# A gated mix of a spectral filter and a state-space scan: a new written order for all five engines

## The chip, the cores and the metric

The kernel runs on one core of one Trainium2 chip. The core has five engines with a queue each: TensorE (PE in the profile, its weight loads PEld), VectorE (DVE), ScalarE (ACT), GpSimd (POOL) and SyncE (SP, which here issues only transfers). The metric is the device time of one execution in microseconds, as the median of three runs. Lower is better. Inputs and outputs are bf16 in HBM.

## The reference

The input x has 2048 tokens of 1024 features. Two branches are computed and mixed by a gate that has one value for each token:

```
g = sigmoid((x * gate_w).sum(-1))
a = irfft2(rfft2(x) * (w_r + 1j*w_i))          # over tokens and features
Bu = x @ B_bar.T ; h[t] = Lam_bar * h[t-1] + Bu[t]   # 1024 complex states, 2048 steps
b = 2 * real(h @ C.T) + x * Dskip
out = g * a + (1 - g) * b
```

Lam_bar and B_bar come from Lambda, log_dt and B. Branch a is the spectral one, branch b the state-space one.

## The kernel before

**Branch b.** Tokens are worked on in 8 chunks of 256. For each chunk four unit steps (unit_mm, L398) multiply the chunk of x with B, 32 matmuls of 128x256 each, into a PSUM tile psu; unit_out (L408) casts it on ACT into the state buffer h. The recurrence on DVE (recur, L347 to L378: rotate, scan, carry, rotate back) is cut into 126 pieces. Then each tile of 128 tokens is multiplied with C: a half-tile step (c_half, L713) is 16 matmuls of 128x512 and fills 512 of the 1024 columns of the PSUM tile ps_y. ACT scales each half by 1 − g into a buffer ye (scale_y, L744; two buffers). For tokens tiles 0 to 9 ("early") SP stores ye to a scratch in HBM (L754), and the skip term x·Dskip is added to it there: DVE multiplies (L769), ACT scales into the buffers su (L779, one pair for all tiles), and POOL issues an accumulating transfer (add_skip, L785). For tiles 10 to 12 ("own") the skip term comes in through four short diagonal matmuls (L719), and POOL adds ye onto branch a with an accumulating transfer (own_add, L884). Tiles 13 to 15 are done last in pieces (c_part, L727) and finished on DVE (L899) and stored (L905).

**Branch a.** The two-dimensional transform goes in steps: transposes of x on PE (L917) and folds on DVE (L943 to L954), a transform over features (fd, L430 to L443, evicted at L449), a first step over tokens (s1, L462, evicted at L474, the last four of 16 into A_last), and a store to a first scratch (L480). From there come 8 tiles Bb in two halves each (load_mid, L508); s2 (L594) transforms them, ACT evicts to X (L603, with one column fixed at L604 by a result of the small chain "middle", L525 to L582), DVE multiplies with W (times_w, L617; W arrives by load_W, L515, four transfers each for w_r and w_i), is1 (L629) transforms back, ACT evicts to C (L637), SP stores to a second scratch (L643). Then come load_last (L651), is2 (L661) with its eviction (L671), and for each token tile the last step (spectral_mm, L806 and L810, into ps_id), scaled by g on ACT (L817), joined on DVE (L825 to L846). POOL adds the scratch of branch b onto it with another accumulating transfer (add_late, L851), and SP stores the result (close, L859).

**Loads.** B is read with transposing transfers (L259), C with 16 of them (load_C, L702), half of these into a region that B or A used before. Db (L758) is Dskip spread over all partitions, xs (L763) a tile of x, K (L497), KRS (L1029) and MT (L499) are constants.

**What sets the order.** No scheduler decides anything: under the manual schedule each engine runs its instructions in the order in which the Python steps emit them. Each step is a generator, each has one letter, and the string ORDER says which generator advances next. The letter v takes the recurrence piece whose number comes next in PIECES. PSUM has four slots, each of the size of a tile of 128x1024 in f32, and SLOTS says which slot the next tile takes; a tile waits until the slot's tile before it has been read for the last time. A transfer of SP is given one of eight counters in turn, and waits until the transfer that had the counter before has landed; POOL's transfers have eight counters of their own.

```
for act in "".join(ORDER):
    if act == "v":
        piece(next(pieces))
    else:
        next(acts[act], None)
```

Letters used below: c load_C, Y load_skip, W load_W, L load_small (K, MT), M load_mid, 3 s2, 4 its eviction to X, n and o the early and own half-tile steps of C, N and O their ye, J the store of ye, h and H the unit step and its eviction, 6 and 7 is1 and its eviction to C, m the su, + the L785, B the L884, Q the L851, l and z spectral_mm and its eviction for tiles 0 to 9, D the store of a finished tile, e the gate's output with the sigmoid (L1014), t the tables with the sines (L1111).

Of the kernel before, what the change touches and what calls it, by code (L numbers as in the profile page):

```python
# [41 lines left out]
S1_DVE = (1, 4, 5)  # L42
CLOSES = (0, 1, 2, 3, 10, 4, 5, 11, 12, 6, 7, 8, 9)
PIECES = (
# [6 lines left out]
)  # L51
SLOTS = (
    "0123012310231023102310230123012031201312031203101230132031231031201312303312013213021021013010320130",
    "1220123203201320130130120321023120320321021023120312301230231201302303120",
)
MIRROR = (6, 7, 8, 9)
ORDER = (
    "xxxTVUVVVaTfVVrrUGTGG|Tfaaa|UafFffftafftUftxFEfTETUFffU22xSEkSTSTArxAfffUAUFTTEUfffUFbxwxbxbbTUEFbfE",
    "1bT~SSUfuFSFAUUUU2bbtbfAF1AtbbtrFttrbEffE11EbEh11SStbttfttttAg1~HtfufhA~tetFSSFrKHrtu1EAvfAEhtttvttt",
    "SSFtbbvvvAtEttH1Avthtftv1cttwv1tcthccctttvtcch~HFtvftHvvhuHtvfStEettStAHhtAeKrvFctcvvFhEEHKtvwtcSvtS",  # L60
    "hvvKc1vcc1vAAKKvv1c1v1hcvswcsLMvvveHHekMYsssnNHvvhHnsvvvJWWMvs3vsvNvvsssssnvssnvvs4NMvv4Njvhv553vhvv",
    "YvyJJL46H4vv5WWvhh5vvvMM78Jj7HHmn3nHvv8M44m6MnN77WW5jv+Yy5vvv3M845+mNY8nMJJMyvvv+467hvHMh5vN7N34vHmh",
    "4J8m+6n3h8v77HmH+55v4n64JMvNnMYy5vW83n+v7N474vJ568vYmmNJ7dh7NWj+v58v5vyvvd88MhvHHm8+MJm6h+n378vv7Hh8",
    "J+d4Y4YX5vv5NnJH6XXv7ny7mNNm8+hn8hvqivvvvvJvqyHihYivvyiqhivqqiYvNImvni+qJJmHIIiini+HinvdIIH+vvIIIqIN",
    "IiiiNmI+vvIInvvImvyJqii%NJINIJYJYmhvvv+vvvlylzvhHmplpzZZH+mZZZhlZvhPPRR++zyRRRlQDQHzRZZmRHZ+ZRZvoOZD",
    "QvlpDzzPovOvQBvZZlpPYvZZvBZDZRDRRRvzQDoloOBzoQOopZOoPOBlzlZRoDDZZvBZZRpQvzCvYZZvZZBZZPRDoQoo9RQQ9yRR",
    "0RRyCooD099C9Y990DD0D0Y00",
)

EVEN = ((0, 0), (2, 1), (2, 0), (0, 1))  # L70
# [1145 lines left out]
```

## Time and profile before

| | |
|---|---|
| median of 3 runs | 305.4 us (304.77, 305.4, 305.66) |
| span of the profiled execution | 303.6 us (the page gives no other time for it) |
| PE busy | 296.4 us (98%) |
| DVE busy | 289.3 us (95%) |
| ACT busy | 188.5 us (62%) |
| POOL busy | 73.3 us (24%) |
| granted TensorE clock | 0.999 |

The span is what lies between the first and the last instruction. A row of a group names the line, the engine, the operation, what is written and read, the count, and then the busy time, the mean duration of one in ns, and the idle time of the engine ahead of these instructions with what ended most of it. In a list by time, a row has start and duration, and a square bracket with the idle time before it. "DMA to landing" is the time from the start of an issue until the last packet has arrived. A wait by engine gives the total, the number of times and the longest.

### The profile page before, as it was taken

The page shows a single profiled execution, that of the slowest core. Times are in us where ns is not written, and L with a number is a line of the kernel's source. Part 1 is how long each engine was busy: PE and PEld are TensorE (multiplying, and loading weights), DVE is VectorE, ACT ScalarE, POOL GpSimd, SP SyncE. Part 2 cuts the span into 40 slices and gives each one's busy share as a digit, 9 for nine tenths or more (in the row PEclk, how much of TensorE's full clock was granted, in tenths as well). Part 3 has the DMA queues.
Part 4 walks back from the last instruction along what each step waited for, and adds up shares of the span by engine and source line. Part 5 has one row for each costly group of instructions (what it writes and reads, how often), then busy time and mean ns, then how long its engine had stood idle before and what let it go on. Part 6 is the DMA issues. An engine that isn't in the chain of part 4 may idle for free. (4 is left out here: it accounts for less than half of the span.)

```text
span 303.6 us, 6402 instructions
## 1 busy us (share of the span) xinstructions
PE 296.4 (98%) x2568; PEld 197.4 (65%) x2592; DVE 289.3 (95%) x340; ACT 188.5 (62%) x255; POOL 73.3 (24%) x99
## 2 busy tenths in 40 slices
PE   8999999999999999999999999999999999999995
PEld 5664677878864685458553866669657986645543
DVE  2999999999999999999999999999899999999995
ACT  4999999896532383667665865529668774343400
POOL 2100420745893001110210220202011253252330
PEclk9999999999999999999999999999999999999999
DMA  6999999989999599895948798687758876978976
GB/s 208 341 201 194 253 193 310 162 142 154 268 214 241 160 259 219 181 250 189 212 96 258 163 223 225 139 294 147 242 174 185 165 88 135 160 132 143 165 153 181
DMA packets 74157, 59.35 MB, mean 196 GB/s; under 512 B 44904, under 2 KB 61680, under 8 KB 74128
## 3 DMA queue, kind: packets, MB, share of 16 engines
q1 hardware_dynamic: 66560, 49.82, 65.8%
q0 software_dynamic: 6912, 8.69, 23.0%
q10 hardware_dynamic: 656, 0.44, 0.5%
q8 instruction: 20, 0.33, 0.4%
q14 instruction: 9, 0.07, 0.1%
HBM read 27.46 MB, written 23.08 MB: 166 GB/s over the span
## 5 line engine op out<-in xcount | busy, mean ns | idle before, releaser
L398 PE MATMUL psu<-xQ,BT 128*128 128x256 bf16 x1024 | 116.5, 273 | 0.2 <-DVE X L449 0.2
L398 PEld LDWEIGHTS <-BT 128*128 128x128 bf16 x1024 | 99.0, 98 | 17.3 <-issue 4.6
L713 PE MATMUL ps_y<-CT,h 128*128 128x512 bf16 x397 | 92.5, 379 | 0.9
L363 DVE TENSOR_TENSOR_SCAN h<-rz,h 128x2048 bf16<-128x2048 f32 (+1 forms) x20 | 70.8, 3561 | 0.0
L713 PEld LDWEIGHTS <-h 128*128 128x128 bf16 x416 | 39.6, 98 | 46.3 <-issue 2.9
L785 POOL DMA_DIRECT2D y_scratch<-su x20 | 17.3, 902 | 135.7 <-ACT su L779 105.4
L408 ACT CAST h<-psu 128x1024 bf16<-128x1024 f32 x32 | 32.3, 1011 | 18.7 <-PE psu L398 13.1
L350 DVE TENSOR_TENSOR h<-h,tab 128x4096 bf16<-128x4096 bf16 (+1 forms) x20 | 37.1, 1859 | 0.1
L744 ACT ACTIVATE ye<-ps_y,omg 128x512 f32<-128x512 f32 x26 | 17.9, 689 | 26.3 <-PE ps_y L713 11.8
L347 DVE TENSOR_TENSOR xQ<-h,tab 128x4096 bf16<-128x4096 bf16 x12 | 27.4, 2284 | 1.0 <-ACT h L408 1.0
L603 ACT CAST X<-ps_s 128x1024 bf16<-128x1024 f32 x16 | 16.2, 1010 | 14.6 <-PE ps_s L594 11.2
L727 PE MATMUL ps_q<-CT,h 128*128 128x512 bf16 (+2 forms) x110 | 21.3, 348 | 0.2
L817 ACT ACTIVATE BT<-ps_id,gB 128x1024 bf16<-128x1024 f32 x14 | 15.3, 1114 | 9.9 <-PE ps_id L810 5.7
L671 ACT CAST ZT<-ps_is 128x1024 bf16<-128x1024 f32 x16 | 15.8, 1017 | 6.2 <-PE ps_is L661 6.2
L637 ACT CAST C<-ps_is 128x1024 bf16<-128x1024 f32 x16 | 15.7, 1011 | 5.1 <-DMA xQ<-in_A_x_dram 3.4
L851 POOL DMA_DIRECT2D BT<-y_scratch x10 | 13.1, 1452 | 19.7 <-DVE BT L846 13.3
L727 PEld LDWEIGHTS <-h 128*128 128x128 bf16 x112 | 10.3, 98 | 10.4 <-DVE h L378 0.5
L779 ACT ACTIVATE su<-xs,omg 128x512 f32<-128x512 bf16 x20 | 14.2, 723 | 4.1 <-DMA y_scratch<-su 2.2
L929 ACT COPY xQ<-pt 128x1024 bf16<-128x1024 bf16 x12 | 12.2, 1082 | 1.3 <-PE pt L919 1.3
L449 ACT CAST X<-ps_fd 128x1024 bf16<-128x1024 f32 x12 | 12.3, 1062 | 1.0 <-PE ps_fd L439 0.9
L617 DVE TENSOR_TENSOR UV<-X,Wb 128x2048 bf16<-128x2048 bf16 x8 | 9.6, 1220 | 0.6 <-ACT ye L744 0.6
L617 DVE TENSOR_TENSOR UV<-X,raw 128x2048 bf16<-128x2048 bf16 x8 | 9.8, 1223 | 0.2 <-ACT X L604 0.2
(200 smaller groups left out, 397.3 us busy)
## 6 DMA issues: line engine op xcount, KB each, us to landing
y_scratch<-ye SPq DMA_DIRECT2D x20, 256.0 KB, 4.6
y_scratch<-su POOLq DMA_DIRECT2D x20, 256.0 KB, 4.7
Bb<-turn_scratch SPq DMA_DIRECT2D x16, 256.0 KB, 5.2
turn_scratch<-C SPq DMA_DIRECT2D x16, 256.0 KB, 4.1
raw<-turn_scratch SPq DMA_DIRECT2D x8, 512.0 KB, 4.3
xs<-in_A_x_dram SPq DMA_DIRECT2D x13, 256.0 KB, 3.9
out_dram<-BT SPq DMA_DIRECT2D x11, 256.0 KB, 4.3
CT<-in_A_x_dram SPq DMA_DIRECT2D x5, 512.0 KB, 6.1
```

The lines of the kernel that those rows point to most:

```text
L347: nc.vector.tensor_mul(out=tmps["s"], in0=u[:, ::-1], in1=bc(i))
L350: nc.vector.tensor_mul(out=u, in0=u, in1=bc(i))
L363: nc.vector.tensor_tensor_scan(out=seg, data0=rz[:, js.start + j:js.start + j + m].rearrange("p j t -> p (j t)"), data1=seg, initial=0.0, ...
L398: nc.tensor.matmul(psu[:, j, :], lhsT=BT[4 * q + j][:, ri, d8, :], rhs=xQ[:, c, d8, :], start=(d8 == 0), stop=(d8 == 7))
L408: nc.scalar.copy(out=hs[c][:, ri, 4 * q:4 * q + 4].rearrange("p b (q j) -> p b q j", j=32), in_=psus.pop((c, q, ri)).rearrange("p b (j q) ...
L603: nc.scalar.copy(out=X2, in_=ps2s[g][b])
L617: nc.vector.tensor_mul(out=UV, in0=X2s.pop((g, b)).unsqueeze(1).to_broadcast([P, 2, 2, K]), in1=fft["Wb"][g // 2 % 2][:, :, at:at + 1, :]. ...
L671: nc.scalar.copy(out=ZT[:, 4 * kp:4 * kp + 4, :, 4 * G:4 * G + 4].rearrange("p (c r) n g -> p c r n g", c=2), in_=pszs.pop((G, kp)).rearra ...
L713: nc.tensor.matmul(psy, lhsT=hs[c][:, ri, jb, P * tq:P * (tq + 1)], rhs=CT[ri][:, jb, 512 * dh:512 * (dh + 1)], start=(i == 0), stop=(i == ...
L727: nc.tensor.matmul(psq, lhsT=hs[c][:, ri, jb, P * tq:P * (tq + 1)], rhs=CT[ri][:, jb, at:at + n], start=(i == 0), stop=(i == 15))
L744: nc.scalar.activation(out=ye, in_=psys[tb][:, K * hf:K * (hf + 1)], func=ACT.Copy, scale=omg[:, tb:tb + 1])
L785: nc.gpsimd.dma_start(out=y_dram[tb, hf], in_=xgs[tb, hf], accum_op=ALU.add)
```

## The change

The three tables PIECES, SLOTS and ORDER get new contents, and nothing else is touched. The letters of ORDER are the same in number, so the same operations are issued, on the same engines, with the same operands, but in another sequence, and PSUM tiles take other slots. The number of activation-table loads on ACT follows from the order: in the old order the last sine comes ahead of the sigmoid, in the new one the sigmoid comes first, and there are four table loads in place of three.

Four stretches of the queues, as they are issued before and after. SP, from the last load of C on:

```
before: C load, K, Bb half 1, KRS, Bb half 2, Db, ye store, W w_r x4, W w_i x4, Bb x2, xs, ...
after:  C load, Db, W w_r x4, xs, K, Bb half 1, W w_i x4, raw w_r x4, Bb half 2, ye store, Bb, ye store, Bb, MT, ...
```

ACT, around the first s2 evictions (h is a unit eviction):

```
before: ... h, h, ye(tile 0), h, h, ye(tile 0), Zr, X, X column, ye(tile 1), X, X column, ye(tile 1), X ...
after:  ... h, h, h, h, ye(tile 0), ye(tile 0), Zr, ye(tile 1), X, X column, ye(tile 1), X, X column, X ...
```

POOL, from its accumulating transfers of branch b on:

```
before: L785 x19, L851 x2, L785, L851 x2, L884 x2 (tile 10), L851, L884 (11), L851, L884 (11), L884 (12), L851, L884 (12), L851 x3
after:  L785 x16, L851 x2, L884 (10), L785, L851 x2, L785, L884 (10), L785 x2, L884 (11), L851 x2, L884 (11), L884 (12), L851, L884 (12), L851 x3
```

PE and ACT at the own tiles. Before, the first ye of tile 10 stands between its two half-tile steps (with two ps_id steps of PE there as well), and tiles 11 and 12 have both half-tile steps ahead of their first ye. After, tile 10 has both half-tile steps first, and the first ye of tiles 11 and 12 stands between the two, with no other step of PE there (in the string: "oOBo" and "oQzQBDDDzRZOZRo"). ACT there, after:

```
after:  ... su(8) x2, ye(10), L817 x2, ye(10), L817 x4, su(9) x2, ye(11), ye(11), L817 x2, ye(12), ye(12), L817 x2
```

The diff:

```diff
@@ -42,29 +42,29 @@
 S1_DVE = (1, 4, 5)
 CLOSES = (0, 1, 2, 3, 10, 4, 5, 11, 12, 6, 7, 8, 9)
 PIECES = (
-    0, 1, 2, 3, 4, 5, 6, 8, 7, 9, 11, 10, 24, 25, 27, 26, 12, 13, 15, 14, 17, 16, 28, 18,
-    20, 21, 19, 23, 22, 30, 37, 38, 29, 40, 39, 50, 41, 31, 33, 34, 43, 35, 36, 42, 51, 44, 46, 45,
-    52, 32, 53, 47, 54, 48, 49, 56, 55, 63, 64, 66, 57, 59, 58, 60, 65, 61, 67, 62, 69, 68, 76, 77,
-    72, 70, 73, 79, 71, 78, 80, 75, 74, 82, 81, 83, 85, 89, 90, 86, 84, 91, 92, 87, 93, 94, 95, 98,
-    96, 88, 99, 102, 100, 103, 97, 104, 105, 106, 107, 108, 101, 111, 109, 112, 114, 113, 115, 116, 110, 118, 117, 119,
-    121, 120, 122, 123, 124, 125,
+    0, 1, 2, 3, 5, 4, 6, 8, 9, 7, 11, 10, 24, 25, 27, 26, 12, 13, 28, 30, 15, 14, 17, 16,
+    29, 20, 18, 21, 23, 22, 37, 38, 19, 39, 31, 50, 40, 33, 34, 41, 35, 42, 43, 36, 46, 44, 47, 51,
+    53, 49, 48, 45, 52, 32, 54, 55, 56, 63, 64, 66, 59, 57, 60, 62, 65, 58, 61, 67, 69, 68, 72, 76,
+    77, 79, 70, 73, 71, 78, 74, 80, 75, 82, 81, 83, 89, 90, 85, 86, 91, 84, 92, 87, 93, 95, 94, 96,
+    88, 98, 99, 102, 100, 103, 97, 101, 104, 105, 106, 108, 107, 111, 109, 112, 113, 114, 110, 115, 116, 118, 117, 119,
+    120, 121, 122, 123, 125, 124,
 )
 SLOTS = (
-    "0123012310231023102310230123012031201312031203101230132031231031201312303312013213021021013010320130",
-    "1220123203201320130130120321023120320321021023120312301230231201302303120",
+    "0123012302130123012301230123012031231023103120310231203201320323103210230201301230123023102302130230",
+    "1230232301302130213021310132013201320321032032102310231023102310321302130",
 )
 MIRROR = (6, 7, 8, 9)
 ORDER = (
-    "xxxTVUVVVaTfVVrrUGTGG|Tfaaa|UafFffftafftUftxFEfTETUFffU22xSEkSTSTArxAfffUAUFTTEUfffUFbxwxbxbbTUEFbfE",
-    "1bT~SSUfuFSFAUUUU2bbtbfAF1AtbbtrFttrbEffE11EbEh11SStbttfttttAg1~HtfufhA~tetFSSFrKHrtu1EAvfAEhtttvttt",
-    "SSFtbbvvvAtEttH1Avthtftv1cttwv1tcthccctttvtcch~HFtvftHvvhuHtvfStEettStAHhtAeKrvFctcvvFhEEHKtvwtcSvtS",
-    "hvvKc1vcc1vAAKKvv1c1v1hcvswcsLMvvveHHekMYsssnNHvvhHnsvvvJWWMvs3vsvNvvsssssnvssnvvs4NMvv4Njvhv553vhvv",
-    "YvyJJL46H4vv5WWvhh5vvvMM78Jj7HHmn3nHvv8M44m6MnN77WW5jv+Yy5vvv3M845+mNY8nMJJMyvvv+467hvHMh5vN7N34vHmh",
-    "4J8m+6n3h8v77HmH+55v4n64JMvNnMYy5vW83n+v7N474vJ568vYmmNJ7dh7NWj+v58v5vyvvd88MhvHHm8+MJm6h+n378vv7Hh8",
-    "J+d4Y4YX5vv5NnJH6XXv7ny7mNNm8+hn8hvqivvvvvJvqyHihYivvyiqhivqqiYvNImvni+qJJmHIIiini+HinvdIIH+vvIIIqIN",
-    "IiiiNmI+vvIInvvImvyJqii%NJINIJYJYmhvvv+vvvlylzvhHmplpzZZH+mZZZhlZvhPPRR++zyRRRlQDQHzRZZmRHZ+ZRZvoOZD",
-    "QvlpDzzPovOvQBvZZlpPYvZZvBZDZRDRRRvzQDoloOBzoQOopZOoPOBlzlZRoDDZZvBZZRpQvzCvYZZvZZBZZPRDoQoo9RQQ9yRR",
-    "0RRyCooD099C9Y990DD0D0Y00",
+    "GVVVVxxxaVaTUTTUUffffftGTG||UffftxVrFFfrakarrtTfffaaE2SxbFEEAUTSArUffTUTUFExxTUTTfUUFFx2SbfffEExASSf",
+    "~fAT1SAkuFfEFUUUUFUAFrEEtgetbbbbbbt11f~ttbffbbueetttEbhHSA2hbttttttt111frrH~tSffuvttvFEFEbbtthAvbvtt",
+    "tf1tttHSASAhfttK11ctttwvvfewttttvttttSAccchhccHe~HHvFESAvttthtFucccFwEvvvvEtHthHSASAvvvvh1Fc1111wScc",
+    "hvtvtEttvccSvAvh1A1cKKcssYvvvvvvsvHHvvKKvHWvKhYssnHvvvNsnNvvvvLsMnssWWMvjsJM3vJnMssLsNyssvs4vvhN5434",
+    "J5vv4MMHvhH677WjhY3Hv54vvvm88n+564vvv7nMyMMM3vJmN7MNh+J5454vHvvn68855WW7nN78vvmJNvvvvv+hHvj6787Yhm34",
+    "4y5vh5HHm+mMvMM3484YynJN867+5W7WM+hXM5344dJmnJ88+HNJnNJ677vjnNY3vvvvh5v45m+4vHv6587588h7yvh86vHhH787",
+    "Hvvmmvnvvddvv8vXqYhnyNiJJvnnIvNNYvJJiIvNhhvHHHqiviqqqyIiIIh+mvi+HvvIiiII+qvvvnivvqJmNviIImnN+viIiinI",
+    "mYiIIqiinIIdv%vvvy++m+m+JvNJllvvvvNhzhHzvYyHpPvYpPZZllZZRhZZRyzzRRZHhHXllRRZoompmJRRJvQQOZZvvDzDzpZZ",
+    "vBOvZZ+QQ+PYppPPyBlvPZZRRvZmZvRvvm++YoOBollODDoQzQBDDDzRZOZRoOBlZZvRzZZvQzZZCYZZRRZZBQQQo9oRR9RRYYDD",
+    "yy00CCDDo9oDD9o900oo90900",
 )
 
 EVEN = ((0, 0), (2, 1), (2, 0), (0, 1))
```

## The prediction

> **What bounds the kernel now.** I read the page's busy times first, then the stretches, the waits of TensorE, and the costliest groups.
>
> ```profile
> PE 296.4 (98%) x2568; PEld 197.4 (65%) x2592; DVE 289.3 (95%) x340; ACT 188.5 (62%) x255; POOL 73.3 (24%) x99
> ...
> PE   8999999999999999999999999999999999999995
> ...
> ACT  4999999896532383667665865529668774343400
> ```
> ```profile
> 0.00:50.00 50.00, 47.20 (x424) 31.93 (x428) 42.48 (x95) 44.22 (x60) 9.01 (x32) 1.00 1.05 241
> 50.00:100.00 50.00, 49.84 (x409) 36.47 (x411) 49.13 (x70) 30.48 (x46) 29.42 (x31) 1.00 1.12 199
> 100.00:200.00 100.00, 99.53 (x967) 62.38 (x975) 99.20 (x78) 61.58 (x89) 10.39 (x12) 1.00 0.82 203
> ```
> ```profile
> PE psw L987 <- DVE A L982: 1.2, 1, 1.2
> ...
> PE psu L398 <- DVE X L449: 0.2, 1, 0.2
> ```
> The second figure of a stretch is the busy time of PE. Of the first 50 us PE idles 2.80, of the next 150 only 0.63. Its waits are six rows of 2.7 us in all, the largest 1.2, the last 0.2. So the kernel is a row of matmuls without gaps. DVE (95%) is nearly as full. No operation is changed, so PE's own work stays, and two things alone can move the time: an order can win back at most the idle of the first 50 us, and every place where the new order lets PE wait adds its wait in full, since nothing later has slack to return it. (303.6 − 296.4 = 7.2 us of idle in all; about 3.2 of it is the tail after the last matmul, by the rows below.)
>
> ```profile
> 292.44 7.99 PE ps_q L727 x52
> ```
>
> Work beside PE, by group:
>
> ```profile
> L398 PE MATMUL psu<-xQ,BT 128*128 128x256 bf16 x1024 | 116.5, 273 | 0.2 <-DVE X L449 0.2
> ...
> L744 ACT ACTIVATE ye<-ps_y,omg 128x512 f32<-128x512 f32 x26 | 17.9, 689 | 26.3 <-PE ps_y L713 11.8
> ...
> L603 ACT CAST X<-ps_s 128x1024 bf16<-128x1024 f32 x16 | 16.2, 1010 | 14.6 <-PE ps_s L594 11.2
> ...
> L817 ACT ACTIVATE BT<-ps_id,gB 128x1024 bf16<-128x1024 f32 x14 | 15.3, 1114 | 9.9 <-PE ps_id L810 5.7
> ...
> L637 ACT CAST C<-ps_is 128x1024 bf16<-128x1024 f32 x16 | 15.7, 1011 | 5.1 <-DMA xQ<-in_A_x_dram 3.4
> ...
> L851 POOL DMA_DIRECT2D BT<-y_scratch x10 | 13.1, 1452 | 19.7 <-DVE BT L846 13.3
> ...
> L779 ACT ACTIVATE su<-xs,omg 128x512 f32<-128x512 bf16 x20 | 14.2, 723 | 4.1 <-DMA y_scratch<-su 2.2
> ```
>
>
> **The change part by part.** I laid the written order against the old one, queue by queue, and looked for steps that now stand behind something which PE itself ends, or behind a long transfer. Five are left.
>
> (a) *Second half of Bb, about 94 us.* In the old SP queue Bb's two halves (L508) came straight after the last C load (L702), and the first s2 step of PE (L594) needs both:
>
> ```profile
> 81.78 1.26 SPq L702 DMA_TRANSPOSE CT<-in_B_C_im_dram  x1
> 83.29 0.36 SPq L497 DMA_DIRECT2D K_sb<-c_K  x1
> 83.75 1.24 SPq L508 DMA_DIRECT2D Bb<-turn_scratch  x1
> ...
> 85.67 0.45 SPq L508 DMA_DIRECT2D Bb<-turn_scratch  x1
> ```
> ```profile
> 93.29 0.62 PE L594 MATMUL ps_s<-Bb,KRS_sb 64*32 64x512 bf16 x16
> ...
> 93.92 3.61 PE L713 MATMUL ps_y<-CT,h 128*128 128x512 bf16 x15
> ...
> 97.39 3.61 PE L713 MATMUL ps_y<-CT,h 128*128 128x512 bf16 x16
> ```
> In the new queue Db (L758), four Wb of w_r, xs, K, Bb's first half, four Wb of w_i and four raw of w_r stand ahead of the second half. The built program gives each SP transfer one of eight counters, so it issues only when the one eight places ahead has landed. That makes a chain of three landings: Db, then the first w_i eight places behind it, then Bb's second half.
>
> ```profile
> Bb<-turn_scratch SPq DMA_DIRECT2D x16, 256.0 KB, 5.2
> ...
> Wb<-in_A_w_i_dram SPq DMA_DIRECT2D x8, 128.0 KB, 5.3
> ...
> Db<-in_B_Dskip_dram SPq DMA_DIRECT2D x1, 256.0 KB, 4.7
> ```
> Sum 15.2 us. Db takes K's place in the queue (issued 83.29), so the half lands at 98.5, later by whatever delays the C loads. They stand behind the A_last stores, which wait for ACT; ACT carries one more table load (below) in its fullest stretch. I allow 2 us (an estimate, bounds 0 and 5): 100.5. PE has one half-tile step of C (L713, 16 matmuls, 93.92 to 97.39, so 3.5) more in front of s2: 93.29 + 3.5 = 96.8. **Stall 3.7.** From below: the shortest landings (3.1 for a W and 3.9 for a Bb, rows below) put it at 83.3 + 4.7 + 3.1 + 3.9 = 95.0, no stall. From above: 5.9 and 6.0 and 5 of delay put it at 104.9, a stall of 8. I take the medians, as three landings in a row rarely all go one way.
>
> ```profile
> L508 SPq DMA_DIRECT2D Bb<-turn_scratch x16: 450/490/1447, 83.8 to 171.4; - x16
> ...
> DMA to landing us min/median/max: 3.9/5.2/6.0
> ```
> ```profile
> L515 SPq DMA_DIRECT2D Wb<-in_A_w_r_dram x8: 332/426/498, 87.4 to 116.1; - x8
> ...
> DMA to landing us min/median/max: 3.1/4.9/5.9
> ```
>
> (a2) *Behind it.* The unit step of PE (L398) after that takes the PSUM slot that the s2 tile leaves. Its eviction (X, L603) is written on ACT behind the ye (L744) of the C half that PE ends just before. So after that half ACT still needs 0.69 + 1.01 before PE goes on, and PE has only one short matmul between. **1.7**; bounds 1.5 and 2.3, as the next row can start 0.1 early or some tenths late.
>
> (b) *About 120 us.* The same form again: a unit step takes the slot of ps_is, whose eviction C (L637) stands behind a ye of the half that PE has just ended. 0.69 + 1.01 − 0.6 of the s2 step (the 0.62 row) = **1.1**, bounds 0.5 and 1.5.
>
> (c) *The end, about 256 to 268 us.* Old rows of this place:
>
> ```profile
> 249.53 0.89 POOL L785 DMA_DIRECT2D y_scratch<-su  x1 [1.80 <-ACT su L779]
> ...
> 254.66 0.39 PE L719 MATMUL ps_y<-xQ 128*128 128x128 bf16 x4
> ...
> 254.88 0.39 PE L806 MATMUL ps_id<-raw,ZT 128*128 128x128 bf16 x4
> ...
> 255.08 0.69 ACT L744 ACTIVATE ye<-ps_y,omg 128x512 f32<-128x512 f32 x1 [3.32 <-PE ps_y L719]
> ...
> 255.54 0.39 PE L806 MATMUL ps_id<-raw,ZT 128*128 128x128 bf16 x4
> ...
> 256.96 1.93 POOL L884 DMA_DIRECT2D raw<-ye  x1
> ```
> The last L785 was done at 250, before the own tiles' ye. Now the last four L785 stand on POOL behind L884 of tile 10, which needs that tile's ye, which needs PE's second half of the tile. On ACT the last two su (L779), which refill the buffers those L785 read, stand ahead of the ye of tile 11's first half. And that ye is now written between tile 11's two halves, so PE's second half (a write into the tile that ye reads) waits for it. The old order has this form at tile 10 only (ye at 255.08), and there two ps_id pairs from 254.88 on cover it, so its trace shows no stall of this kind. From PE's end of tile 10: ye 0.69, L884 1.28 (mean of four, row below), the first L785 0.89, L851 twice 1.45, the second L785's landing 4.7, su 0.72, ye 0.69 = 11.9 us. (The second L785 of tile 8 stands behind the two L851; the landing is counted from the start of its issue.) PE has between: five ps_id pairs of 0.66 (254.88 to 255.54, two L806 starts) and a C half of 3.5 with its diagonal 0.2 (254.66 to 254.88) = 7.0. **Stall 4.9.** The landing's ends give 3.8 and 7.6:
>
> ```profile
> L785 POOL DMA_DIRECT2D y_scratch<-su x20: 845/857/1126, 117.0 to 249.5; - x20
> ...
> DMA to landing us min/median/max: 3.6/4.7/7.4
> ```
> ```profile
> L884 POOL DMA_DIRECT2D raw<-ye x4 | 5.1, 1276 | 3.8 <-ACT ye L744 3.8
> ```
> (d) *Tile 12*: the same inversion with nothing else queued: ye 0.69 and the hand-over: **0.8**, bounds 0.5 and 2.7 (if an L817 ahead of it waits for a store).
>
> *At nothing:* the extra table load. The sigmoid (L1014) now comes ahead of the last sine (L1111), so ACT loads four times, not three:
>
> ```profile
> L1111 ACT ACT_TABLE_LOAD x1 | 1.3, 1283 | 0.0
> ```
> 1.28 us of ACT near 60 us, where the slices show it at 9; what it delays on PE is swallowed by (a), whose wait follows. If (a) is not there it costs up to 1.3. [...] On DVE the W products (L617) may wait for their loads and hold the recurrence pieces behind them; I cost it at nothing, since DVE idles 303.6 − 289.3 = 14 us in all and every stall of PE gives it as much again. The moved early steps (T2, G, B loads) I cost at nothing, bounds −2.8 (all idle of the first 50 us gone) and +2.
>
> **Sum.** 3.7 + 1.7 + 1.1 + 4.9 + 0.8 = 12.2 us. Against the profiled span 303.6 that is 315.8; the median of the runs, 305.4, is 1.8 over that span (no other time of that execution is shown), so 317.6, say **317.5**.
>
> **Rivals.** *Only the tail and the slots stall* (a = 0, because landings go short): 305.4 + 8.5 = 313.9. For it: the W loads are small; against: three landings in a row. *Everything goes late*: a = 8, c = 7.6, d = 2.7: 305.4 + 21.1 = 326.5. For it: the DMA share in that stretch is already above 1, so more W in a row may stretch landings; against: the maxima come from single rows. *Faster*: the start. The new head of the order closes the 2.8 us of PE's idle in the first 50 us: 305.4 − 2.8 = 302.6 at best. It decides only where (a) to (d) sum to less than 1.9 us (2.8 − 0.9). For it: the first steps are the most moved; against: (a2), (b), (c) and (d) all start from an end of PE itself, so PE cannot outrun them. [...]
>
> **How the numbers follow.** Forecast as summed (four or five stalls) 0.58; tail and slots alone 0.20; everything late 0.12; faster 0.07; no change 0.03. 0.3% (0.9 us) is about what a measurement of this kernel tells from no change. Range: the low end takes in the second case with the shortest tail (313.9 − 1.1 = 312.8) and something regained at the start (−2.8): 310. The high end stands 6 us over the forecast, between it and 326.5: 324. Faster 0.07, same 0.03, slower 0.90.
>
> **What would show it.** PE's waits get rows: L594 on Bb near 97 us (3 to 4), L398 on X L603 and on C L637 (1 to 2 each), L713 on ye L744 near 265 (about 5) and 275 (about 1). PE's busy time stays at 296. The digits of PE drop in the slices at 13 and 34 or 35. Wrong: no PE wait above 1 us after 90 us; or a stall in a place not listed, above all between 125 and 245 us, where I found none; or PE waiting on DVE.

## The result and the profile after

The new order takes 326.8 us (median of four, 324.5 to 329.8) against 305.1 before; the ratio is 1.068, interval 1.063 to 1.072. (A ratio leaves out an execution that is over 1.5% above the fastest of its kernel: 329.8 here, 322.9 in the first experiment.) It is slower, as forecast, but by 21.7 us and not by 12.2: the time lies 2.8 us above the range. Its executions also differ by 5 us among themselves, those of the old order mostly by 1 to 2.

Page of the new order, lines that answer to those of before:

```profile
PE 301.5 (93%) x2569; PEld 197.3 (61%) x2592; DVE 292.2 (90%) x340; ACT 189.0 (58%) x256; POOL 79.0 (24%) x99
...
PE   8899999999986799899999999999999997488996
...
PEclk9999999999998899999999999999999999979999
```

The waits of PE in the new order (total, times, longest):

```profile
PE ps_y L713 <- ACT ye L744: 6.5, 2, 5.7
PE ps_s L594 <- DMA Bb<-turn_scratch: 2.7, 1, 2.7
PE psu L398 <- ACT X L603: 1.7, 1, 1.7
PE ps_s L462 <- ACT X L449: 1.5, 1, 1.5
PE ps_id L806 <- ACT BT L817: 1.4, 2, 1.2
PE psw L987 <- DVE A L982: 1.2, 1, 1.2
PE psu L398 <- ACT C L637: 1.1, 1, 1.1
PE psu L398 <- DMA BT<-in_B_B_im_dram: 1.0, 2, 0.7
PE ps_y L713 <- DMA Wb<-in_A_w_r_dram: 0.9, 1, 0.9
```

All rows of this view, with the four small ones left out here, sum to 19.0 us; before, the six rows gave 2.7. That is 16.3 us of new waiting. PE is also busy for 5.1 us more (301.5 for 296.4) with the same matmuls. Together that is 21.4, and the span grew by 21.3. So the whole loss is on PE, in two parts: it waits, and some of its matmuls take longer. Every wait that the prediction named has a row, with a size within about 1 us of the forecast. The second part was not forecast. It shows in the row PEclk, where slices 13, 14 and 36 dip, and in PE's list by time around the two longest waits:

```profile
99.97 0.39 PE L594 MATMUL ps_s<-Bb,KRS_sb 64*32 64x512 bf16 x1
103.09 0.62 PE L594 MATMUL ps_s<-Bb,KRS_sb 64*32 64x512 bf16 x15 [2.73 <-DMA Bb<-turn_scratch]
103.64 5.31 PE L713 MATMUL ps_y<-CT,h 128*128 128x512 bf16 x16
...
110.68 1.58 PE L398 MATMUL psu<-xQ,BT 128*128 128x256 bf16 x13 [1.71 <-ACT X L603]
```
```profile
275.90 3.61 PE L713 MATMUL ps_y<-CT,h 128*128 128x512 bf16 x15 [0.18 <-ACT BT L817]
279.35 0.39 PE L719 MATMUL ps_y<-xQ 128*128 128x128 bf16 x4
285.39 5.01 PE L713 MATMUL ps_y<-CT,h 128*128 128x512 bf16 x16 [5.65 <-ACT ye L744]
```

A half-tile step of C takes 3.6 us elsewhere, 5.31 behind the first of these waits, and 5.01 behind the second: 1.7 and 1.4 us more. Stretches of 3.41 us ahead of and behind the end of each wait show why (the last three figures are granted clock, DMA share, GB/s):

```profile
100.52:103.93 3.41, 0.84 (x17) 0.31 (x18) 3.38 (x9) 0.00 (x0) 0.00 (x0) 1.00 1.03 289
103.93:107.34 3.41, 3.41 (x10) 1.22 (x9) 1.68 (x1) 0.00 (x0) 0.00 (x0) 0.50 0.74 222
...
281.42:284.84 3.42, 0.00 (x0) 0.00 (x0) 3.42 (x3) 0.80 (x2) 0.00 (x0) 1.00 1.13 178
284.84:288.25 3.41, 2.86 (x7) 1.01 (x7) 3.41 (x3) 0.50 (x1) 3.19 (x4) 0.50 0.80 195
```

PE was busy for 0.84 us of the first stretch and for nothing of the third; each time it runs at half clock through the 3.41 us behind.

And POOL's list at the end:

```profile
271.56 0.90 POOL L884 DMA_DIRECT2D raw<-ye  x1 [11.34 <-ACT ye L744]
272.12 1.23 POOL L785 DMA_DIRECT2D y_scratch<-su  x1
272.68 3.15 POOL L851 DMA_DIRECT2D BT<-y_scratch  x2
274.14 2.64 POOL L785 DMA_DIRECT2D y_scratch<-su  x1
...
279.15 0.89 POOL L785 DMA_DIRECT2D y_scratch<-su  x1 [1.49 <-ACT su L779]
```
with ACT beside it,
```profile
277.70 0.77 ACT L779 ACTIVATE su<-xs,omg 128x512 f32<-128x512 bf16 x1
284.04 0.72 ACT L779 ACTIVATE su<-xs,omg 128x512 f32<-128x512 bf16 x1 [5.57 <-DMA y_scratch<-su]
284.67 0.67 ACT L744 ACTIVATE ye<-ps_y,omg 128x512 f32<-128x512 f32 x1
```

The second su waits for the L785 issued at 274.14 until 284.0, so that transfer took 9.8 us, the maximum of its view ("DMA to landing us min/median/max: 4.0/5.7/9.8"); the prediction had 4.7, and 7.4 as the upper end. Then come su and ye, and PE goes on at 285.39.

Five things were to be told apart: whether the tail chain is what was described, why the L785 took 9.8 us, whether idle time is what lowers the clock, whether the waits simply add, and what is left when they are undone.

### The profile page after: what moved, and what is told of

It is laid out like the page before. It is cut to its first block, busy times and chain, and to the rows that moved or that the text cites. A ratio compares the mean times of both kernels' runs of the same rounds, so it can differ in the third digit from the quotient of the medians.

```text
span 324.9 us, 6404 instructions
## 1 busy us (share of the span) xinstructions
PE 301.5 (93%) x2569; PEld 197.3 (61%) x2592; DVE 292.2 (90%) x340; ACT 189.0 (58%) x256; POOL 79.0 (24%) x99
## 3 DMA queue, kind: packets, MB, share of 16 engines
q0 software_dynamic: 6912, 8.69, 21.7%
## 5 line engine op out<-in xcount | busy, mean ns | idle before, releaser
L398 PE MATMUL psu<-xQ,BT 128*128 128x256 bf16 x1024 | 116.8, 273 | 3.9 <-ACT X L603 1.7
L398 PEld LDWEIGHTS <-BT 128*128 128x128 bf16 x1024 | 98.5, 98 | 23.4 <-issue 9.3
L713 PE MATMUL ps_y<-CT,h 128*128 128x512 bf16 x398 | 95.7, 388 | 8.6 <-ACT ye L744 6.5
L713 PEld LDWEIGHTS <-h 128*128 128x128 bf16 x416 | 40.5, 100 | 57.3 <-issue 14.8
L785 POOL DMA_DIRECT2D y_scratch<-su x20 | 19.7, 1021 | 146.6 <-ACT su L779 120.4
L744 ACT ACTIVATE ye<-ps_y,omg 128x512 f32<-128x512 f32 x26 | 17.8, 688 | 55.3 <-PE ps_y L713 26.5
L851 POOL DMA_DIRECT2D BT<-y_scratch x10 | 14.0, 1733 | 19.1 <-ACT BT L817 12.1
L817 ACT ACTIVATE BT<-ps_id,gB 128x1024 bf16<-128x1024 f32 x14 | 14.8, 1123 | 4.0 <-PE psu L398 4.0
L727 PEld LDWEIGHTS <-h 128*128 128x128 bf16 x112 | 10.4, 98 | 10.5
L671 ACT CAST ZT<-ps_is 128x1024 bf16<-128x1024 f32 x16 | 15.4, 1021 | 1.2 <-PE ps_is L661 1.2
L449 ACT CAST X<-ps_fd 128x1024 bf16<-128x1024 f32 x12 | 11.8, 1009 | 1.9 <-PE ps_fd L439 1.7
L347 DVE TENSOR_TENSOR su<-h,tab 128x2048 bf16<-128x2048 bf16 x8 | 10.1, 1267 | 1.8 <-ACT X L449 1.4
```

Source lines behind the costliest of these rows:

```text
L347: nc.vector.tensor_mul(out=tmps["s"], in0=u[:, ::-1], in1=bc(i))
L398: nc.tensor.matmul(psu[:, j, :], lhsT=BT[4 * q + j][:, ri, d8, :], rhs=xQ[:, c, d8, :], start=(d8 == 0), stop=(d8 == 7))
L671: nc.scalar.copy(out=ZT[:, 4 * kp:4 * kp + 4, :, 4 * G:4 * G + 4].rearrange("p (c r) n g -> p c r n g", c=2), in_=pszs.pop((G, kp)).rearra ...
L713: nc.tensor.matmul(psy, lhsT=hs[c][:, ri, jb, P * tq:P * (tq + 1)], rhs=CT[ri][:, jb, 512 * dh:512 * (dh + 1)], start=(i == 0), stop=(i == ...
L727: nc.tensor.matmul(psq, lhsT=hs[c][:, ri, jb, P * tq:P * (tq + 1)], rhs=CT[ri][:, jb, at:at + n], start=(i == 0), stop=(i == 15))
L744: nc.scalar.activation(out=ye, in_=psys[tb][:, K * hf:K * (hf + 1)], func=ACT.Copy, scale=omg[:, tb:tb + 1])
```

## The experiments

### The tail: two L785 ahead of the first L884

```diff
-DzpZZvBOvZZ+QQ+PY
+DzpZZv++BOvZZQQPY
```

> Two L785 of tile 8 are moved on POOL to ahead of the first L884, nothing else. Theory (the stall of PE near 280 us comes from the landing of the second of them, 9.8 us behind two L851 in POOL's queue, and the half clock after it comes from the long idle): the wait of L713 on ye falls from 5.7 to about 0.8, the half clock of about 3 us after it goes, 326.8 - 5 - 1.4 = about 320.5. Rival (the ye of tile 11 is late for another reason, its place behind four L817 on ACT): the wait stays above 4, time 325 to 327. Rival (the half clock is a matter of time in the run or of DMA load): wait gone, clock still 0.50 for some us there, about 322.

Measured: 319.35 us, ratio 1.045 (1.041 to 1.049) against 1.068 (1.063 to 1.072): 7.5 us less. The rows of PE at that place:

```profile
PE ps_y L713 <- ACT ye L744: 2.5, 3, 0.9
PE psu L398 <- ACT X L603: 1.7, 1, 1.7
PE ps_s L594 <- DMA Bb<-turn_scratch: 1.6, 1, 1.6
```

The longest wait on ye fell from 5.7 to 0.9, and the row PEclk of this run has no dip anywhere. The chain of the prediction holds: moving two issues on POOL, an engine busy for 24%, undoes it. Not all of the 7.5 us is this edit's. The wait on Bb, 170 us ahead of it, was 1.6 in this execution and no half clock followed, so at its first wait on L817 behind tile 10 PE was already earlier by 2.9 us (269.44 in place of 272.31). From there to its last matmul it gained another 6.2, and 1.5 were lost again between that matmul and the end of the span (4.7 us in place of 3.2).

### The tail: only behind the two L851, or also behind L884

```diff
-vZZ+QQ+PY
+vZZ++QQPY
```

> The new order with one L785 moved by two places on POOL: the second of tile 8 stands ahead of the two L851, and still behind the first L884. Theory (it landed after 9.8 us because the two L851 issued just ahead of it hold POOL's one queue): it lands in about 5 us, at 278.5, before PE ends the first half of tile 11 (279.6), and the wait of L713 on ye falls from 5.7 to about 0.9, as in the run with both moved: about 319.5. Rival (it was slow from the load on DMA in that stretch, or from its place behind L884): it still lands near 283, 325 to 327.

```profile
271.69 0.90 POOL L884 DMA_DIRECT2D raw<-ye  x1 [11.34 <-ACT ye L744]
272.25 2.13 POOL L785 DMA_DIRECT2D y_scratch<-su  x2
273.36 3.51 POOL L851 DMA_DIRECT2D BT<-y_scratch  x2
```
```profile
279.49 0.39 PE L719 MATMUL ps_y<-xQ 128*128 128x128 bf16 x4
280.70 3.61 PE L713 MATMUL ps_y<-CT,h 128*128 128x512 bf16 x16 [0.82 <-ACT ye L744]
```

Measured: 323.1 us, ratio 1.055 (1.045 to 1.064). The moved transfer landed 6.3 us after its issue, at 279.1, and the wait at this place fell to 0.82. So the place behind the two L851 made it slow: POOL's transfers landed in the order of their issue (in the new order's trace those issued at 272.12, 272.68, 273.40, 274.14 and 274.71 us at 276.8, 280.3, 282.9, 284.0 and 284.9). The time fell by 3.8 only, half of the forecast. That had taken the 7.5 of the run above whole; and what was moved from the front went to the back of the same queue. The two L851 landed after 8.8 and 10.1 us and the L884 of tile 11's first half after 10.1; the ye of tile 12, which takes the buffer that this L884 reads, held PE for 1.9 us.

### The head: Bb's second half directly behind the first

```diff
-vLsMnssWWMvj
+vLsMMnssWWvj
```

> The issue of Bb's second half is moved on SP to directly behind the first half, ahead of eight W loads. Theory: it lands some 5 us earlier (98 in place of 103), PE does not wait for it at 100 us (2.7 gone) and no stretch at half clock follows (1.7 gone); the wait of L398 on X behind it stays at 1.7. 326.8 - 4.6 = about 322. Rival (what PE lost there comes back as a wait for W at L617 or for raw at L629): 324 to 326. Rival (the half clock has another cause than the idle): 324 with 0.50 still in the rows.

Measured: 326.1 us, ratio 1.069 (1.064 to 1.075), no change that can be told. In its profile the wait on Bb is gone and L713 behind it takes 3.63. Bb's second half landed at 100.7, but PE came to it only at 104.3, so this profile alone does not show that the edit removed the wait. (The run with four edits and two ye below does: PE came at 100.1, the half had landed at 97.6, and PE did not wait.) The wait for B near 50 us grew from 1.0 to 3.5 in this execution, and a dip of the clock is seen there (the digit 7 of PEclk in the slice from 48.7 to 56.8 us):

```profile
PE ps_y L713 <- ACT ye L744: 7.4, 3, 5.7
PE psu L398 <- DMA BT<-in_B_B_im_dram: 3.5, 1, 3.5
```

That wait stands 45 us ahead of the edit, so the edit did not make it: the load that PE waited for was issued at 42.85 and landed at 52.45, after 9.6 us, where it took 5.3 in the profile of the new order. A gain of some microseconds at one place is lost in that spread, and what this edit alone is worth stays open.

### Work in place of idle time

```diff
             ps2 = [psum([P, 2, K], "ps_s2") for _ in range(2)]
+            for i in range(14 if g == 0 else 0):
+                nc.tensor.matmul(ps2[1][:, i % 2, :], lhsT=ident, rhs=xQ[:, 7, 0:2, :], start=True, stop=True)
```

> Fourteen matmuls of 128x512 that nobody reads are added on PE just ahead of the first s2 step, into the PSUM tile that it fills next, so PE works while Bb's second half is under way; its landing is not touched. Theory of idle and clock: PE is not idle for 3 us, the clock stays at 1.00, the L713 step after it takes 3.6 in place of 5.3: about 325. Rival (the clock falls for another reason, such as load on DMA or DVE in that stretch): the step still takes 5.3, 326.5 to 327.5.

```profile
99.75 3.18 PE L592 MATMUL ps_s<-xQ,ident 128*128 128x512 bf16 x14
102.86 0.63 PE L596 MATMUL ps_s<-Bb,KRS_sb 64*32 64x512 bf16 x16
103.42 3.63 PE L715 MATMUL ps_y<-CT,h 128*128 128x512 bf16 x15
```

With PE at work through the same wait, the step behind it takes 3.63 in place of 5.31, at a granted clock of 1.00. DMA and DVE are as loaded as before (from 100 to 103 us a DMA share of 1.00 against 1.06, and DVE busy for 2.97 us in both). The time, 327.9 us (ratio 1.070 to 1.082), does not show the 1.7 us; it is if anything longer, within the spread of 326.2 to 330.6.

### Two ye behind the evictions that free a slot

```diff
-sLsNyssvs4vvh  ...  MM3vJmN7MNh
+sLsyssvs4Nvvh  ...  MM3vJm7NMNh
```

> On ACT two ye are moved to behind the eviction that frees a PSUM slot: ye of tile 1 behind the first X, ye of tile 2 behind the C of the same stretch. Theory: the waits of L398 on X (1.7) and on C (1.1, with hand-over 1.3) go: 326.8 - 3.0 = about 324. Rival (the slots are held by something else just as long, or the moved ye make the next step wait): 326 to 327.

Measured: 325.4 us, 1.4 less and half of the forecast, but with the same ratio, 1.068 (1.065 to 1.071), so it is not resolved. Both rows, L398 on X and L398 on C, are gone from the waits, so the cause of (a2) and (b) is shown. The profiled execution gave part of it back at waits for transfers that the edit does not move: 1.5 on BT in place of 1.0, 3.0 on Bb in place of 2.7, and 0.6 each for K and for x, which had no row.

### The kernel before, with Bb's second half behind the W loads

```diff
-HHekMYsssnNHvvhHnsvvvJWWMvs
+HHekYsssnNHvvhHnsvvvJWWMMvs
```

(The second letter M of the string moves from behind k to behind WW; the letters around it stay.)

> The kernel before, with one step put as in the new order: the issue of Bb's second half stands on SP behind the eight W loads. Theory: it is issued near 92 and lands near 97.2, PE waits for it at 93.3 for 3.9 us, and since PE is idle that long, about four us at half clock follow, 1.7 more: 305.0 + 5.6 = about 310.6. Rival (idle alone does not lower the clock): 309 with 1.00 in the rows. Rival (the W loads are small and the half lands in time): 305.

```profile
92.66 0.39 PE L594 MATMUL ps_s<-Bb,KRS_sb 64*32 64x512 bf16 x1
97.49 1.05 PE L594 MATMUL ps_s<-Bb,KRS_sb 64*32 64x512 bf16 x15 [4.44 <-DMA Bb<-turn_scratch]
...
98.55 5.82 PE L713 MATMUL ps_y<-CT,h 128*128 128x512 bf16 x15
```

Measured: 308.4 us, ratio 1.012 (1.006 to 1.019). In the profiled execution PE waits 4.4 us, the next steps run at half clock (0.50 from 97 to 103 us), and it takes 312.2. The others took 307.75, 307.8 and 309.0, at mean clocks of 1.0, 1.0 and 0.994. So the misplaced transfer cost 2.7 us in the executions at a clock of 1.0 and 7 in the one at 0.989: whether the clock held differed between executions of one program.

> The kernel before with Bb's second half behind the W loads, as the first run of that kind (four executions of 307.75, 307.8, 308.96 and 312.19 us at clocks of 1.0, 1.0, 0.994 and 0.989), and twenty matmuls of 128x512 that nobody reads ahead of the first s2 step, so PE works through the wait. Theory (idle lowers the clock): clock of 0.998 or more in all executions, no stretch at 0.50 in the profile, all within 1.5 us of each other near 308.5. Rival (another cause): executions at 0.99 and 312 are still seen.

That run adds, in the way shown above, twenty matmuls to this kernel. All four executions have a clock of 1.0, and around this place its profile has no step above 3.7 us: with PE at work through the wait, none ran at half clock. They lie between 309.3 and 311.6, median 310.2: wider apart than expected (the profiled one waited 1.0 for B near 51 us), and the twenty matmuls take 4.5 us themselves, about as much as the wait. The clock held here, at 1.0 against 0.989 to 1.0 without them, but it is no gain.

### Three loads of B ahead of three stores

```diff
-hbttttttt111frrH~tSffuvttvFEFEbbtthAvbvttt
+hbtttttttfrrH~tSffuvttvFEFEbbtthAvb111vttt
```

> The last three loads of B are moved on SP to ahead of three stores that stood before them, nothing else. Theory: the wait of L398 on BT near 50 us (1.0 to 3.5 by execution, and half clock where it is longest) goes, and with it a part of the spread between executions: 326.8 - 1.6 = about 325, spread below 3 us. Rival (the loads are late because of the load on DMA, not their place): wait still there, 326 to 327.

Measured: 327.0 us, ratio 1.072 (1.068 to 1.076); the wait on BT is 0.9, where it was 1.0. The first of the three loads was issued at 42.22 in place of 43.82, but landed at 49.38 in place of 49.07. The rival's forecast holds: the place behind these stores is not why they are late. What is stays open. The executions spread over 2.5 us, as the theory had it, but with the wait still there four of them do not show that the edit did it.

### The edits together

> Four edits of the new order together: the two L785 of tile 8 ahead of the first L884, Bb's second half behind the first, two ye behind the evictions, three loads of B ahead of three stores. Theory (stalls of PE simply add): 326.8 - 7.5 (measured for the first alone) - 4.6 - 3.0 - 1.6 = about 310; left over are the waits for the last load of C (0.9), for L817 (2) and for ye of tiles 11 and 12 (2). Rival (undoing one stall uncovers another, as DVE, 95% busy before, becomes the bound): 314 or more, with waits of PE on DVE.

> As the run with the four edits, and the first ye of tiles 11 and 12 are moved behind the second half-tile step of their tile. Theory: the two waits of L713 on ye (0.9 each) go: about 1.8 below that run, near 308. Rival (the slot or the sum on POOL is then late, and PE waits there): the same as that run.

Measured: 315.9 us (1.030 to 1.040) and 315.2 us (1.030 to 1.038). The four edits take 10.9 us off, where the 7.5 measured for the first and the forecasts of the others add to 16.7. That sum counts the head twice, as 2.9 of the 7.5 lay there, and it has 1.6 for the loads of B, whose move brought nothing. The two ye take hardly anything more, though their waits are gone. PE's waits in the second of these runs are short, the longest being

```profile
PE ps_s L462 <- ACT X L449: 1.5, 1, 1.5
PE ps_id L806 <- ACT BT L817: 1.4, 2, 1.2
PE psw L987 <- DVE A L982: 1.2, 1, 1.2
PE ps_y L713 <- DMA Wb<-in_A_w_r_dram: 0.9, 1, 0.9
```

Its span is 9.1 us longer than that of the order before. PE is idle for 4.5 us more between its matmuls and busy for 1.5 us more, and the other 3.1 lie behind PE: the span ends 6.3 us after its last matmul (at 306.5), where before it ended 3.2 after. The last L851, issued at 298.19, landed at 308.64, and SP's last stores stood behind the store that waits for it. So there was a second bound under the stalls of PE, and the rival's number came true, but not its cause: in the run with four edits PE waits on DVE for 1.2 us, as in the order before, and for 0.7.

> As the run with the four edits and the two later ye, and two kinds of waits of DVE are taken out as well: the two unit columns (L609), which waited 1.9 and 0.9 for W, stand just ahead of the products that need them, and the first ye of tile 10 stands on ACT behind the two L817 that DVE (2.3) and PE (1.2 and 0.2) waited for. Theory (with PE's stalls undone, DVE sets the end, so that run stood at 315 in place of 308): the end comes 5 earlier on DVE and 2 earlier on PE, about 310. Rival (the end is set elsewhere, in the stores or in POOL's sums): 314 to 315.

Measured: 313.6 us (1.020 to 1.033), 1.6 less than without these last edits and 3.6 above the forecast. In the profiled executions the span is 0.6 shorter. DVE's waits for W are gone there, but it still waits 1.9 us for L817 and now 1.6 for PE, so this run hardly tests what DVE's waits cost. The end is set on POOL here too. Its last row is

```profile
296.39 2.45 POOL L851 DMA_DIRECT2D BT<-y_scratch  x2 [3.08 <-issue]
```

The second of these landed at 308.0, after 10.9 us, and the stores behind it on SP could not issue before. PE's last product ended at about 306, and the span is 312.1. So the rival of that run was nearer: with most of PE's waits out of the way, POOL's accumulating transfers carry the end here, the last of them landing 4.1 us ahead of it. No version came near the order before, so the comparison with it is not taken further.

## Why the prediction was wrong

**Direction and places** were right. Each of (a), (a2), (b), (c) and (d) is a row of the waits or of the list by time, and undoing (a), (a2) and (b), and (c), took their rows away. The forecast sum of these terms is 12.2 us; measured they are 2.7 + 1.7 + 1.1 + 7.2 + 0.8 = 13.5.

**(a)** was built rightly and sized a little high, 3.7 against 2.7. The chain of three landings was 4.2 + 5.9 + 5.3 = 15.4 us (forecast 15.2), as SP's rows show:

```profile
87.60 0.52 SPq L758 DMA_DIRECT2D Db<-in_B_Dskip_dram  x1
...
91.83 2.16 SPq L515 DMA_DIRECT2D Wb<-in_A_w_i_dram  x4
...
97.76 0.45 SPq L508 DMA_DIRECT2D Bb<-turn_scratch  x1
```
It began 2.3 us later than assumed, since the C loads ended later than the allowance of 2. But PE came later too, at 100.0 and not 96.8, since the early steps, costed "at nothing", lost 3.2 us, by the waits 1.5 on L449 at 12 us, 1.0 on B and 0.9 at 92 us. (The trace names a W load as what ended the last of these. In the run with Bb moved the same wait of 0.86 stands against ye L744: it is the ye between the two halves of tile 0, the form of (d), which the prediction looked for at the own tiles only.) Together they set when s2 goes on: at 103.09, where the forecast had 100.5. The two are not independent, as Db's issue waited in the end for PE itself (0.6 us, for L544). The bound of +2 for the early steps was too small.

**(a2), (b), (d)**: 1.71, 1.1 and 0.8 us against 1.7, 1.1 and 0.8. These waits, a fixed sequence of ACT rows behind an end of PE, were priced to a tenth here.

**(c)** was mis-sized, 4.9 against 7.2 (5.65 before the second half, 1.4 and 0.2 ahead of it where L817 stood behind ye and PE waited for a slot). The term that failed is "the second L785's landing 4.7": it measured 9.8, 5.1 more. The stall is off by 2.3 only, because from PE's end of tile 10 to the issue of that transfer 3.6 us went by in place of the 5.8 put for ye, L884, L785 and two L851, and PE had 7.7 us of work in place of 7.0. That these made up for half of the error is luck. The 4.7 came from twenty transfers of which nineteen had no L851 shortly ahead, and the upper end of 7.4 from the same rows. In its new place right behind two L851 the transfer landed when these had, after 9.8; moved ahead of them in one run, after 6.3. The trace of before held the sign: its last L785, issued at 249.53, landed at 255.3, just after the L851 issued at 246.01, which landed at 254.0.

**What was missing** is the clock: 1.7 + 1.4 = 3.1 us. The trace of before has no idle time of PE above 1.2 us between its matmuls, so no row of it showed this, but the forecast put idle times of 3 to 5 us into the order and priced them as waiting alone. Its sign "PE's busy time stays at 296" failed (301.5).

In the trace of the new order the clock was 0.50 from 103.93 to 107.34 us and from 284.84 to 288.25, for 3.41 us each, and the row PEclk has no other dip; the two falls lie 180.91 us apart, which is 53 times 3.413. In the kernel before with Bb's second half moved it was at 0.50 for 6.8 us, twice as long (mean clocks of 0.92 from 92 to 97 us, 0.50 from 97 to 103, 0.99 from 103 to 105). The 3.41 us ahead of the two falls of the new order had 0.84 and 0.00 us of matmuls in them; the 3.41 us from 278.01, with 1.73 us of matmuls, had full clock behind them. (The ends of matmuls are modelled, so these times are not known to the hundredth.) Counted in steps of 3.41 us from the falls, the place of a gap told the cases below apart, and not its length. A gap of 1.87 us was followed by half clock in the run with one L785 moved; it lay inside one step, which had 1.54 us of matmuls:

```profile
100.87:104.28 3.41, 1.54 (x22) 0.56 (x21) 3.38 (x9) 0.18 (x1) 0.00 (x0) 1.00 1.04 313
104.28:107.69 3.41, 3.41 (x10) 1.23 (x9) 1.43 (x1) 0.00 (x0) 0.00 (x0) 0.50 0.54 169
```

One of 3.02 us was not in the run with the two ye moved; it lay across two, with 1.68 and 2.08 us of matmuls (steps counted back from the later fall of that run, at 281.33):

```profile
100.42:103.84 3.42, 1.68 (x9) 0.69 (x8) 2.04 (x2) 0.18 (x1) 0.00 (x0) 1.00 1.11 232
103.84:107.25 3.41, 2.08 (x22) 0.84 (x23) 3.38 (x9) 1.01 (x1) 0.00 (x0) 1.00 1.06 317
```

The steps at this wait begin at another time in each of the three profiles (103.93, 104.28 and 103.84 us), which fits that executions of one program differ. Of the executions without a profile only the mean clock is on record, so for them this is argued and not shown.

**The rivals.** "Everything late" gave 326.5, close to the time but for other reasons: (a) was 2.7 and not 8, (d) 0.8 and not 2.7. The chance of 0.12 for it was low because the sum held only terms that could be read from rows of before. "Faster" and "no change" (305.4) fell with the first wait: the span grew by 21.3 us, PE's waits and its busy time by 21.4, so no stall of PE was absorbed.

Of the 21.3 us between the two profiled spans, 13.5 are the five terms, 3.4 the early waits, and 3.1 the clock. So of the 9.1 us by which the forecast fell short, the terms that were in the sum make 1.3, the early waits that were put at nothing 3.4, and the clock 3.1. The remaining 1.3 are 2.0 of busy time of PE that the clock does not explain, less small waits of before that are gone; no run here separates them. Why the loads of B land so differently between executions also stays open.

## What to carry to other kernels

When a change puts idle time on a full PE, price it twice: once as waiting, and once for the clock behind it: here 1.7 and 1.4 us, for 3.41 us at half clock each time, behind stretches of 3.41 us with 0.84 and 0.00 us of matmuls. The shortest gap seen with half clock behind it was 1.87 us, the longest with full clock behind it 3.02. One L785 landed after 9.8 us behind two L851 and after 6.3 ahead of them, where the median of its kind was 4.7 before. So price a transfer by its place in its queue too: where it moves behind others, add theirs. And look for an accumulating or reading step between two writes of the same tile all along the order, not only where the diff is densest.

## What was not expected of the hardware

- The granted clock of the new order went to 0.50 twice between its matmuls, for 3.41 us each (103.93 and 284.84 us), behind stretches of 3.41 us with 0.84 and 0.00 us of matmuls. In the profiles of these runs, gaps of 1.87, 2.40, 2.73 and 3.5 us and longer ones were followed by half clock, and gaps of 1.56, 1.71, 1.92 and, once, 3.02 us were not; four executions of one program had mean clocks from 0.989 to 1.0 (312.2 to 307.75 us).
- Accumulating transfers issued by POOL in a row landed in the order of their issue: 4.6, 7.6, 9.4, 9.8 and 10.2 us after their issues, for five issued within 2.6 us (272.12 to 274.71 us of the new order's trace); the one issued just ahead of them took 3.0.
